# A new hand-laid order for a fused attention and token-mixing kernel

## The chip, the cores and the metric

The kernel runs on one core of a Trainium2 chip. A core has five engines with instruction queues of their own, each working strictly in order: TensorE (PE: matrix products and transposes, written to PSUM), VectorE (DVE), ScalarE (ACT), GpSimd (POOL, which does not read PSUM here), and SyncE (SP), which in this kernel issues all transfers (DMAs). The metric is the device time of one launch in microseconds. Three launches of the kernel before took 235.21, 235.92 and 237.58 us; the median is 235.92 us.

## The reference

Inputs are q, k and v (8 batches, 8 heads, 576 positions, 64 per head) and four weights. The first half is an attention in two parts whose results are added:

```python
# coarse: means over 4 neighbouring positions, full softmax over 144, result repeated 4 times
out_up = np.repeat(sm_attn(q_d, k_d, v_d), 4, axis=2)
# local: softmax over the positions with |i - j| < 4
mask = np.abs(pos[:, None] - pos[None, :]) < 4
scores = np.where(mask, 0.125 * q @ k.T, -1e9)
x = out_up + softmax(scores) @ v          # then heads are laid side by side: 8 x 576 x 512
```

The second half mixes tokens and channels:

```python
theta = x @ w_theta
y = w_tok_r @ (x * cos(theta)) + w_tok_i @ (x * sin(theta))     # over the 576 positions
u = x + y
out = u + np.maximum(u @ w_ch, 0)
```

Everything comes in and goes out as float32; inside, the kernel computes in bfloat16 with float32 sums.

## The kernel before, in words

One launch works through the eight batches. A batch is cut into steps of some tenths of a microsecond to one microsecond each, and each step has a two-letter name:

- `lk`, `lq` load a pair of heads of k or q into one of 16 staging slots (line 287); `ck`, `cq` cast it to bfloat16 (line 296); `tp` transposes it on PE (line 303), `ev` moves it from PSUM (line 316). Batch 7 is transposed by DMA instead (`dk`). `kd`, `qd` sum groups of four positions (lines 322 to 336). `lv`, `lw` load v (line 348), `cv` casts it (line 396). For batch 0, v takes another way (`l1`, `c1`, `t1`, `e1`, `x1`).
- Coarse attention: `pv`/`vd` (means of v), `sd` (scores, line 426), `ed` (exponential, line 437), `nd` (line 447), `xn` (normalising, line 458), `xd` and `xc` (transposed to xdT, lines 466 and 470).
- Local attention: `ps` (scores, line 482), `ex` (exponential, line 490), `mk` (product with the band, line 501), `po` (line 511), `nm` (normalising, lines 519 and 520), `xt` (transpose, line 533), `xa` (sum of both attentions, line 541).
- Second half: `th`, `tt` (x times w_theta, lines 552 and 564), `cs`, `ct` (cosine and sine), `xm` (x transposed, line 591), `zz`, `zt` (products), `mx` (token matrices, line 632, eight steps of nine matmuls per batch), `ua` (x + y, line 637), `up`/`uc` or `du` (u transposed by PE or by DMA), `ch` (u times w_ch, line 662), `rl` (line 667), `st` (store, line 671). The last 64 positions of two batches go together through `ut`, `dt`, `ht`, `rt`, and are stored by `sr` and `ss` (line 700).
- Weights: `la`/`ca` theta, `lb`/`cb` the token matrices with their transposes `wp`/`wc` (line 273), `lc`/`cc` the channel weight.
- `wm` issues matmuls of a constant tile whose result nobody reads (line 755): its first character is a PSUM bank, the second a number of 512-column matmuls, the third a last one in units of 64 columns. `te` and `ts` make ACT load the table of the exponential or of the sine early (line 761). `k0` does nothing.

A string, `ORDER`, holds 1,191 such words and is the whole schedule. The program takes the words one by one; each kind of word goes through its batches and parts by itself (the first `tp` is batch 0's first, and so on), and what stands behind the two letters says where: a letter v, a or g is the engine (DVE, ACT, POOL), a digit or two are PSUM banks, and for loads a character is the staging slot:

```python
    for word in ORDER.split():
        kind, place = word[:2], word[2:]
        ...
        STEPS[kind][0](*next(todo[kind]), place)
        pin()
```

`pin()` ties each instruction to the one before it on the same engine, so every engine's queue, SP's too, has exactly the order of the words. Between engines the waits come from the data: a step starts when its inputs are there and its buffer or bank is free. In the text, `tp111` is the `tp` step of batch 1, head group 1, q (the last digit is 0 for k, 1 for q), and `lq13` the fourth load of q of batch 1.

Of the kernel before, what the change touches and what calls it, by code (L numbers as in the profile page):

```python
# [67 lines left out]
lv9 tp23 nm ts cs cqa th4 lq7 xm5 xt01 th6 evv cs tp23 xa zz cqa tt4 ua tp01 kdg cs ct cqg evv ztv th5 lw evv lw xm7
zz cs tp23 mx6 xm4 kdg zp5 qdg ua eva zz cvv ps01 cqa ps23 lv8 xm7 kdg zz zcv lk4 te ex lw mx6 mx4 ua mx5 sd01 mkv lvb
lw ua ex po67 mkv cva ps23 qdg lca lcc utg ed lce nm mx4 cvg ex lcd lvf ua lk1 po01 lk2 sd67 lw po23 ckg nm cqa nm mx5  # L70
ckg ed tp01 cvg ua lq5 eva tp67 mx4 lq0 cca ua up5 evv cvg ua ccg ccg pv23 mkg ucv vda lk3 qdv ps01 ps67 ex up4 mx5
ccv nd23 ex ua nd01 uca kdg ch5 po67 xn ps23 ckg cka lv9 mx4 xn tp01 lw ex mkg rl nm lk6 cva ckg xd5 sd23 ua cqg xcv
# [12 lines left out]
po01 ch4 zz lw cs nm zz ztg ch7 te ex dz xd6 ch5 cvg rl lw lqe utg rl mkg po01 ps23 st mx4 lw lkd up7 cqg cka st ex
up2 uca nm ch3 rl xt01 kdg st st cvg xcv cva qdg ckg ua xa mkg uca po45 pv67 mx2 nm mx0 ua lk6 sd45 vda lk2 rl lq7
xt67 cqg ua ps23 xa mx1 lv5 ed po45 ua lq3 nm st mkv cqg dt ex dk9 sd23 xt67 ckg ed mx0 mkg du xa nd45 ch1 ckg ua po23
xn po67 th0 ts cs th4 tt5 nm cs nd23 rl dkf nm ct cqg evg dka xm1 xm0 mx6 zz th1 th7 cs dk1 cs xm4 xm5 zz ztv xn ua zz
mx6 zz mx4 po23 ua dz xt01 po67 xd5 ua xcv eva lw evg mx4 nm st mx5 eva du xa mx2 ht3 qdg ua mx4 xt01 ua kdg nm ua utg
ps67 du rt cvv du st ps23 kdg ua te ex ex mx5 mx4 ps67 lvb lv0 lw lw qdv xa lv8 sd23 cva xt01 ua mkv xa mkg mx5 ex st  # L90
lv4 ua po67 ua ed nm sd01 ed po23 mkg cvg ch4 ch5 mx0 nm tt1 lw lw cvg cvg rl sr po67 rl dxd po23 ua nm po45 nm ts ct
nm th0 pv67 th1 dx vda ch2 ztg nd45 st st nd67 du xn du xn cs cs du th3 cs th0 xd1 xt45 xt67 rl xcv cs xt23 xa utg dxc
ch1 dx zz ch0 ch4 xa ss ch5 dz th6 zz ch7 dt du xa tt2 zz th3 dxe dx zz st cs rl th1 mx6 cs mx3 ct st ua rl ztv rl cs
dx7 dx mx2 th6 ht4 rt zz mx1 ua mx0 cs rl mx3 mx6 zz dz rl zz ua ua zz mx7 mx1 mx2 ua ua mx0 ua mx3 ua mx6 ua ua mx1
st ua du mx0 st mx2 ua ss utv ch3 ua ua ua st ua utv ch2 ch1 ch0 ch7 ch6 du ch4 du du du du st rl sr rl du du rl dt
ch1 st st rl st rl st st rl rl ht0 rl st st rm su rt sr ss st
"""


# [699 lines left out]
```

## Time and profile before

| what | value |
|---|---|
| three launches, us | 235.21, 235.92, 237.58 (median 235.92) |
| profiled execution: span, us | 232.1 |
| median less the profiled span, us | 3.8 |
| PE busy | 220.7 us (95%), of which 40 dummies of 512 columns are 10.6 us |
| DVE, ACT, POOL busy | 191.8, 156.1, 135.5 us |
| DMA queue of the kernel | 84.6% of 16 engines' time, 48.81 MB |
| transfers issued by SP | 197 plain and 36 transposes |

The profile shows one execution. The page gives its span alone, from the first to the last instruction; what lies around it is in the timed launches only. A row of the page's groups reads: line, engine, operation, tile written, tiles read, shape, count, then the busy time of the group and the mean of one in ns, then the idle time of the engine just before, with what ended it. Busy time counts overlapping instructions once; PE's matmuls overlap their neighbours, so a mean is longer than the spacing.

### The profile page before, as it was taken

The page shows a single profiled execution, that of the slowest core. Times are in us where ns is not written, and L with a number is a line of the kernel's source. Part 1 is how long each engine was busy: PE and PEld are TensorE (multiplying, and loading weights), DVE is VectorE, ACT ScalarE, POOL GpSimd, SP SyncE. Part 2 cuts the span into 40 slices and gives each one's busy share as a digit, 9 for nine tenths or more (in the row PEclk, how much of TensorE's full clock was granted, in tenths as well). Part 3 has the DMA queues.
Part 4 walks back from the last instruction along what each step waited for, and adds up shares of the span by engine and source line. Part 5 has one row for each costly group of instructions (what it writes and reads, how often), then busy time and mean ns, then how long its engine had stood idle before and what let it go on. Part 6 is the DMA issues. An engine that isn't in the chain of part 4 may idle for free.

```text
span 232.1 us, 9462 instructions
## 1 busy us (share of the span) xinstructions
PE 220.7 (95%) x3986; PEld 153.2 (66%) x3986; DVE 191.8 (83%) x365; ACT 156.1 (67%) x241; POOL 135.5 (58%) x179
## 2 busy tenths in 40 slices
PE   7998899999998999999999999999999998999991
PEld 2665678777776765776768766676676563767750
DVE  6699999989997988868997997799889967567572
ACT  3359999799877989867976979857766591620000
POOL 7468989869999656897472837767386510000000
PEclk9999999999999999999999999999999999999998
DMA  6999989999999899989606895899957766556676
GB/s 204 382 392 390 298 134 252 365 263 193 264 263 195 224 290 208 203 209 210 174 3 178 226 234 147 293 249 173 153 122 189 144 138 100 154 126 182 138 235 217
DMA packets 76795, 49.41 MB, mean 213 GB/s; under 512 B 61136, under 2 KB 61392, under 8 KB 76752
## 3 DMA queue, kind: packets, MB, share of 16 engines
q1 hardware_dynamic: 76752, 48.81, 84.6%
q8 instruction: 31, 0.51, 1.1%
q14 instruction: 12, 0.10, 0.2%
HBM read 33.98 MB, written 9.44 MB: 187 GB/s over the span
## 4 chain that ended last, share of the span: by engine, by line
PE 72%; DVE 12%; DMA 5%; SPq 3%; issue 3%; ACT 2%; DVEq 0%
PE PS L632 24%; PE PS L662 10%; PE PS L552 9%; PE PS L303 5%; PE PS L755 4%; PE PS L511 3%; DVE xT L541 3%; DMA out_dram<-osb 2%; DVE pm L501 2%; PE PS L591 2%; PE PS L482 2%; DMA st<-xT 2%; SPq L641 2%; PE PS L533 2%; DVE uT L637 2%
## 5 line engine op out<-in xcount | busy, mean ns | idle before, releaser
L632 PE MATMUL PS<-WT,z 128*128 128x288 bf16 x576 | 77.9, 286 | 1.7 <-issue 1.7
L632 PEld LDWEIGHTS <-z 128*128 128x128 bf16 x576 | 53.8, 98 | 17.5 <-issue 2.8
L637 DVE TENSOR_TENSOR uT<-PS,xT 128x288 bf16<-128x288 f32 x64 | 28.1, 450 | 11.4 <-PE PS L632 11.1
L552 PE MATMUL PS<-wth,xT 128*128 128x512 bf16 x128 | 32.3, 380 | 0.7 <-DVE xT L541 0.7
L557 ACT ACTIVATE cs<-PS,pihc 128x512 bf16<-128x512 f32 x32 | 22.3, 696 | 15.1 <-PE PS L552 9.9
L662 PE MATMUL PS<-wch,uT 128*128 128x512 bf16 (+1 forms) x132 | 30.6, 373 | 0.0
L520 DVE TENSOR_TENSOR tmp<-PS,rl 128x512 bf16<-128x512 f32 x40 | 27.7, 692 | 1.4
L541 DVE TENSOR_TENSOR xT<-PS,xdT 128x928 bf16<-128x928 f32 (+1 forms) x24 | 22.7, 952 | 3.4 <-PE PS L533 3.1
L490 ACT ACTIVATE pm<-PS 128x1024 bf16<-128x1024 f32 (+1 forms) x24 | 20.4, 877 | 7.0 <-PE PS L482 2.7
L501 POOL TENSOR_TENSOR pm<-pm,band 128x1024 bf16<-128x1024 bf16 (+1 forms) x13 | 22.2, 1709 | 2.9 <-ACT pm L490 2.9
L667 DVE SCALAR_TENSOR_TENSOR osb<-PS,ur 128x512 f32<-128x512 f32 (+1 forms) x33 | 21.8, 669 | 2.4 <-PE PS L662 1.6
L330 POOL TENSOR_TENSOR two<-kT 128x580 f32<-128x580 bf16 x15 | 17.5, 1163 | 6.1 <-ACT kT L316 5.2
L296 POOL CAST q_tm<-st 128x576 bf16<-128x576 f32 x22 | 14.4, 664 | 10.8 <-DMA st<-in_q_dram 10.8
L662 PEld LDWEIGHTS <-uT 128*128 128x128 bf16 x132 | 12.2, 98 | 12.2 <-issue 0.3
L558 ACT ACTIVATE cs<-PS 128x512 bf16<-128x512 f32 x32 | 19.4, 605 | 0.0
L330 POOL TENSOR_TENSOR two<-qT 128x576 f32<-128x576 bf16 x11 | 12.8, 1167 | 10.5 <-ACT qT L316 7.1
L552 PEld LDWEIGHTS <-xT 128*128 128x128 bf16 x128 | 11.2, 98 | 10.7 <-issue 1.3
L616 DVE TENSOR_TENSOR z<-PS,cs 128x1024 bf16<-128x1024 bf16 x24 | 16.2, 685 | 1.9 <-PE PS L591 0.9
L437 ACT ACTIVATE pd<-PS 128x864 bf16<-128x864 f32 x16 | 14.1, 889 | 5.2 <-PE PS L426 5.2
L761 ACT ACT_TABLE_LOAD x13 | 16.7, 1283 | 0.2
L296 POOL CAST k_tm<-st 128x576 bf16<-128x576 f32 x21 | 14.4, 695 | 1.4 <-DMA st<-in_k_dram 1.4
L396 POOL CAST v_w<-st 128x512 bf16<-128x512 f32 x21 | 13.3, 653 | 1.3 <-DMA st<-in_v_dram 1.2
(119 smaller groups left out, 419.3 us busy)
## 6 DMA issues: line engine op xcount, KB each, us to landing
st<-in_q_dram SPq DMA_DIRECT2D x32, 288.0 KB, 6.3
st<-in_k_dram SPq DMA_DIRECT2D x32, 288.0 KB, 6.0
st<-in_v_dram SPq DMA_DIRECT2D x70, 128.0 KB, 4.7
out_dram<-osb SPq DMA_DIRECT2D x31, 256.0 KB, 2.9
out_dram<-osb SPq DMA_DIRECT2D x10, 128.0 KB, 2.4
st<-in_v_dram SPq DMA_DIRECT2D x4, 288.0 KB, 3.7
st<-in_moe_w_tok_r_dram SPq DMA_DIRECT2D x4, 288.0 KB, 6.2
st<-in_moe_w_tok_i_dram SPq DMA_DIRECT2D x4, 288.0 KB, 7.2
```

The lines of the kernel that those rows point to most:

```text
L296: COPY[w](out=to[:, r, :], in_=of[:, r, :])
L330: nc.gpsimd.tensor_tensor(out=t, in0=src[:, :, 0:2], in1=src[:, :, 2:4], op=ALU.add)
L490: nc.scalar.activation(out=pm[(3 * b + u) % NPM][:, :, 0:n].rearrange("p e c j w -> p e (c j w)"), in_=at.pop(("ps", b, u))[:, :, 0:4 * W ...
L501: EW[w].tensor_tensor(out=t, in0=t, in1=m, op=ALU.mult)
L520: nc.vector.tensor_tensor(out=tmp[(NCH * b + c) % NTMP].rearrange("p g (j d) -> p g j d", d=D), in0=ps[:, :, :, 0:D], in1=r.unsqueeze(3).t ...
L541: nc.vector.tensor_tensor(out=xT[b % 2][:, :, lo:lo + cnt].rearrange("p e (m j) -> p e m j", j=4), in0=at.pop(("xt", b, u))[:, :, 0:cnt].r ...
L552: nc.tensor.matmul(out=ps, lhsT=xT[b % 2][:, dc, P * c:P * c + P], rhs=wth[:, dc, :], start=(dc == 0), stop=(dc == 3))
L557: nc.scalar.activation(out=t[:, 0, :], in_=ps, func=AF.Sin, bias=pihc, scale=1.0)
L632: nc.tensor.matmul(out=ps, lhsT=z[b % 2][:, j, P * dc:P * dc + P], rhs=WT[:, j, cols], start=(j == 0), stop=(j == 8))
L637: nc.vector.tensor_tensor(out=uT[b % 2][:, dc, cols], in0=at.pop(("mx", b, i)), in1=xT[b % 2][:, dc, cols], op=ALU.add)
L662: nc.tensor.matmul(out=ps[:, cols], lhsT=uT[b % 2][:, dc, P * c:P * c + P], rhs=wch[:, dc, cols], start=(dc == 0), stop=(dc == 3))
L667: nc.vector.scalar_tensor_tensor(out=o[:, cols], in0=at["ch", b, c][:, cols], scalar=0.0, in1=ur[b % 2][:, c, cols], op0=ALU.max, op1=ALU.add)
```

## The change

Only the string `ORDER` is another one. It has the same 1,191 words in number, and the same steps, with these differences that can be counted:

| words | before | after |
|---|---|---|
| `wm` (dummies) | 8: 40 x 512 + 1,984 columns | 6: 24 x 512 + 1,152 columns |
| `te`, `ts` (table loads) | 6, 7 | 7, 8 |
| `ck`, `cq` on DVE / ACT / POOL | 1 / 20 / 43 | 12 / 15 / 37 |
| `cb` on DVE / ACT / POOL | 0 / 1 / 8 | 2 / 0 / 7 |
| `cv` on DVE / ACT / POOL | 8 / 11 / 21 | 7 / 12 / 21 |
| `mk` on DVE / POOL | 11 / 13 | 9 / 15 |
| `kd`, `qd` on DVE / POOL | 6 / 26 | 5 / 27 |
| `xc` on DVE / ACT | 7 / 1 | 2 / 6 |
| `uc` on DVE / ACT | 6 / 10 | 8 / 8 |
| `ev` on DVE / ACT / POOL | 9 / 21 / 2 | 8 / 21 / 3 |

The loads of q, k and v, the weights and the stores are issued in another order and into other slots. Of the 16 slots the new order uses 14. The start, a part of the middle and the end of the diff:

```diff
@@ -55,45 +55,45 @@
 ORDER = """
-l10 l11 l12 c1v c1a c1g k0 l13 kcv wm061 t101 c1g lq4 e1v wm256 t123 lk5 lk6 kca e1v wm483 x12 x13 lk7 ckv lq8 x10 cka
-lq9 x11 tp45 kcg cqa cva cqg x16 cqg lka cvv cvv lqb evv cvv ckg cva lkc kdg cka cqa lqd ckg lke laf wm772 tp23 evv
-wm754 tp67 pv45 tp01 qdv kcg eva vdv la0 kdg lq1 eva cka wm256 ps23 ex ps67 lk2 qdv ps01 mkv wm446 sd45 sd23 ex ed
...
-cbg lw cbg cqg lw xa xm1 nm th6 xt23 lv6 evv th7 ts cs xa zz tp45 cbg cbg wp0 cs wcv lv3 xm6 cs tt2 xm3 th7 wp1 lw xm0
-zz zz lw qdv lk8 wcv eva ct lk4 lq9 cs cbg cbg cbg cbg wp6 wca wp3 wp2 wp4 wp5 wca wp1 wcv wcv wcv wp2 ztg ps67 ps45
...
-ch1 st st rl st rl st st rl rl ht0 rl st st rm su rt sr ss st
+l10 l11 l12 c1a c1v c1a wm760 t101 l13 c1a wm765 t123 e1v e1a kcv kcv lk4 lk5 ckg lq6 cqg lq7 lk8 ckv wm735 tp01 x12
+kcg kcg x13 x14 x15 eva cvv lk0 x16 lq9 lq1 cqg wm720 tp01 ckg lq2 cvv lk3 lk4 ckg cva cva kdv cva cqg pv23 eva lq5
+cqv tp45 tp01 evv la6 qdg lka kdv vda eva wm752 ps01 la8 ps23 ckg cka ex qdv tp45 mkv cag ex cqv wm726 sd67 cqg ed mkg
...
+xca ckg ckg xt23 mkg tp01 lb6 lb2 xa xt67 caa ts lb5 po45 cbg th2 lb8 xa nm cbg cbg cbg evv cs xm3 xm7 th6 cs cbg xt45
+cbv th2 cs lb0 wp0 wp6 xa wcv wca cbg cbg wp1 zz lq1 tt4 kdg lqa th0 lv9 wp6 cbv lv4 wp5 wp3 ct wcv lv3 cqg cqg cs
+tp12 lv6 lw eva lw lw lw zz wcv lv2 lw xm4 xm6 wp7 wcv ztg wcv lka lk1 lq0 lq8 zz zp0 zca wp5 wp4 lk5 qdg zz qdg wcv
...
+rl st st ch0 rl st st st rl rm st st su ht7 rt sr ss k0
 """
```

Around the tail stores of the first two batches the old order reads `ht0 cka ed rt ... ps67 ss ...` with `sr` much later, the new one `ht7 ex up6 lv3 uca rt sr up0 ...` with `ss` much later.

More of the change, by code (lines that the diff above doesn't have):

```diff
@@ L68 @@
[L68 to L72, printed above, removed]
@@ new lines @@
+ztv lcb eva tp23 zz ucv zp5 th4 cs ckg lv1 lw lv2 lvc ckg xm6 evv mx0 cka cs te zcv xm7 tp12 ckv zz zz qdg kdg cvv lw
+ps34 ex ua ps56 ex mx7 qdg evv mkv ua mx0 ua cca cqg tp12 eva up5 ucv mx7 ua po56 sd01 lw mx2 kdg cvg sd34 cva cvg lc4
+ed nm mkv ps01 lc5 ua ex po56 ed cvv cvg up7 lq6 lk3 lk8 uca lq1 lva lw mx2 ccv lq2 lqb nm po01 po34 nm lv7 pv56 mx7
+lk9 nm tp01 cvg lkc lv0 ua lw lw ccv mkg vda nd56 nd23 xn xn eva ua mx4 ua ps01 ps56 po23 nm xd7 cca ch4 xcv rl qdg ex
+ex xt01 cqv sd23 ed ps67 xa lv6 lv5 lv4 lvd ex mkg mx5 ua cqv xt23 xt67 xa po01 nm lw lw xa th4 kdg ckg ch5 lw rl cva
@@ new lines @@
+ts up3 th2 cs xm4 xm7 ckv ckv ckg up6 uca tt3 cs lqc st tp01 zz utg uca th2 th4 evv zz ct po56 st sd01 lq9 nm lv8 xm3
+cs cs te lk3 xm2 ch7 zz lk1 rl cvg cvg pv45 ed ztg zz lk0 lk7 up3 zp6 zca cqg ch7 ch2 st cqa uca vdv rl lw tp01 rl eva
+st nd45 cva tp67 xn nd23 xn cvv lw tp01 qdg cqv lqc ch5 st rl st ch2 eva xd7 eva mkg mkg po01 po56 xca rl nm nm ps34
+ex kdg qdg mx2 mx0 mkg ua ua ps67 lv5 cva lk4 ex xt23 xa sd45 ckg mx0 utv xt67 xa po23 ua nm cvg cvg ed sd45 cqa ed ts
+kdg lq3 mx1 ua tp67 evv th0 cs mx2 th1 xt67 ua lv9 lw cqa cs lv8 po45 cqg xa nm lw lw pv02 vda xm3 mx7 qdg ua zz tt4
@@ new lines @@
+th0 nd23 xn ct xm7 th1 dt zz lvc lw ckg cs xm0 nd23 tp67 tp45 lq3 lqd lq6 cs lk1 lkb up1 mkg lq2 lva eva xn xm2 cvg
+lv5 zz eva te zz ucv mx3 ua po67 po01 nm nm ztv qdg ps45 st xd2 ex mkv lw mx3 cqa ua ch7 xt01 ps56 ps34 rl xca ex xa
+zp2 zcv ht7 ex up6 lv3 uca rt sr up0 ucv st ch1 utg po67 kdg sd23 ed sd45 ed cqg cka ckv ch0 nm lw rl mkg ps67 lk7 lkd
+ex po23 ckg lw mx1 nm po23 cvg cva ts po45 xt67 rl cvg ua xa mx0 mkg nm nm th1 lv4 lv9 lw lv8 lvc up7 ua cs ucv cva
+mx2 mx3 xt01 ua po45 cqg pv27 ckg nm xa lq0 ua ckg ckv ch6 rl cqg ss vda tp45 tp01 dk7 eva evv th7 cs qdg nd23 lq2
@@ new lines @@
+tp45 eva xm6 lw tp01 lw xm7 xn cva th2 zz zz eva evg tt3 ct cs xm7 nd56 xn mx0 ua zz th3 mx0 ztv ps12 ua ps67 cs po34
+nm lqa kdg cqa te cqg xm0 mx5 zz cvg ex ua mx3 up5 ex kdg xd4 up2 up1 ch0 ua mkg st st ch3 uca lw xca qdv rl uca sd45
+ed lv5 lw ucv xt67 dz xa xt01 utg mx2 cka lq0 xa cvg mx7 mx0 lv7 cvv rl ps34 ex cvg cvg sd56 ed ua ua ua po12 st mx7
+nm st ua xt01 xa lv8 mkg po56 nm pv23 vda up7 ch4 mkg cqa cqg mkv dkc lkd ckg up0 uca ts ucv lv4 ch5 nd23 dkd dka nd67
+rl tt4 ct rl th5 cs du du xn po01 po23 xn po67 nm nm evg eva th4 th5 evg xm3 xm2 zz nm th0 cs cs ztg zz xm1 mx3 mx4 ua
@@ new lines @@
+ua xm2 xd3 xcv mx7 qdg lw cs te po34 lw lw zz zz dz ps56 ex xt01 ua xa ht2 nm mx7 ua utv ps01 ps34 ex ex xt56 xa mx7
+ua ch0 rl cva dt mx7 xt01 rt sr xa mkg cva ts cvg ua kdg po34 po56 st du st mx2 tt7 nm du nm mx0 ua ua mx6 kdg qdg
+sd45 mkv po23 cvv st st sd01 ct te ed ed nm mx7 mx5 pv01 ua ztg ua po67 mkg po23 ua mx5 ua dx4 du ss du du dx nm ch4
+rl dx7 nm vda ts nd01 xn th5 cs th7 cs nd23 xn ch4 rl ch0 xd7 dx xt12 xt34 xt56 xca rl xa xa xa zz dz zz st st uta th0
+du ch7 ch1 ch2 dt cs zz tt0 th6 ct th5 th0 ch3 ch4 rl cs zz th6 mx7 rl st ua ztg cs rl mx5 ht7 mx2 mx1 dx5 dx cs cs
```

35 lines of the change are left out of this document (7 added, 28 removed).

## The prediction

> **What bounds the kernel now.** I read the page first: its busy line, and the DMA lines in 40 slices of 5.80 us.
>
> ```profile
> span 232.1 us, 9462 instructions
> PE 220.7 (95%) x3986; PEld 153.2 (66%) x3986; DVE 191.8 (83%) x365; ACT 156.1 (67%) x241; POOL 135.5 (58%) x179
> DMA  6999989999999899989606895899957766556676
> GB/s 204 382 392 390 298 134 252 365 263 193 264 263 195 224 290 208 203 209 210 174 3 178 226 234 147 293 249 173 153 122 189 144 138 100 154 126 182 138 235 217
> ```
>
> TensorE (PE) is busy for 95% of the span, but the DMA digits stand at 8 or 9 from 5.8 to about 104 us. The averages hide which of the two leads where, so I next read the stretches: microseconds, then busy time (instructions) of PE, PE's weight loads, DVE, ACT and POOL, the granted clock, the DMA share and GB/s.
>
> ```profile
> 20.00:35.00 15.00, 13.26 (x329) 10.19 (x328) 14.49 (x28) 14.95 (x24) 13.06 (x17) 1.00 0.98 253
> 35.00:50.00 15.00, 14.96 (x396) 12.03 (x395) 13.91 (x30) 12.99 (x20) 11.82 (x16) 1.00 1.01 299
> 50.00:65.00 15.00, 14.99 (x292) 10.82 (x283) 14.54 (x23) 14.08 (x24) 14.29 (x18) 1.00 1.11 234
> 65.00:80.00 15.00, 13.87 (x373) 10.82 (x374) 13.04 (x26) 11.30 (x17) 12.72 (x16) 1.00 0.99 216
> 80.00:100.00 20.00, 19.45 (x352) 13.39 (x354) 15.95 (x34) 16.94 (x27) 15.13 (x19) 1.00 1.10 243
> 100.00:120.00 20.00, 20.00 (x373) 13.85 (x361) 17.19 (x32) 17.23 (x28) 14.79 (x20) 1.00 0.66 156
> 120.00:140.00 20.00, 19.76 (x413) 14.68 (x412) 17.83 (x31) 15.04 (x25) 9.25 (x11) 1.00 0.73 192
> 140.00:160.00 20.00, 20.00 (x428) 13.38 (x426) 16.78 (x33) 15.11 (x24) 15.12 (x19) 1.00 1.00 219
> 160.00:180.00 20.00, 19.40 (x379) 14.31 (x377) 18.09 (x31) 14.70 (x19) 12.46 (x11) 1.00 0.80 160
> 180.00:200.00 20.00, 19.21 (x298) 10.97 (x298) 15.11 (x30) 10.91 (x20) 3.71 (x6) 1.00 0.64 124
> ```
>
> Three things follow. PE has little left to win: from 35 to 200 us its idle time is 0.04 + 0.01 + 1.13 + 0.55 + 0.24 + 0.60 + 0.79 = 3.4 us. From 20 to 80 us four resources are close to full at once: the DMA engines (0.98 to 1.11), PE, and DVE with 14.49 + 13.91 + 14.54 + 13.04 = 56.0 of 60 us. And in the first 20 us PE looks full only because the order puts dummy matmuls (words `wm`, line 755) where it expects PE to wait. The granted clock is 1.00 in all of these rows, so it is no term here.
>
> **The change, part by part.** Every step runs as before, on the same tiles; what changes is the order, the engine of some copies, masks and sums, the staging slots, the PSUM banks, the number of table loads and the dummies. PE's real work is therefore the same.
>
> *Fewer dummies.* The eight old `wm` words have 40 matmuls of 512 columns and 1,984 columns in remainders, 22,464 columns; the six new ones have 24 and 1,152, so 13,440. The rate comes from two words of the old order, 8 x 512 + 192 = 4,288 and 5 x 512 + 256 = 2,816 columns:
>
> ```profile
> 8.31 1.97 PE L755 MATMUL PS<-warm 128*128 128x512 bf16 x9
> 14.27 1.35 PE L755 MATMUL PS<-warm 128*128 128x512 bf16 x6
> ```
>
> 0.62 us for 1,472 columns is 0.421 ns each, and 9,024 columns fewer are 3.8 us off PE's queue. That is worth 3.8 us only if what follows on PE is ready 3.8 us sooner.
>
> *What is late next: landings.* A load's median time to landing against the spacing of the issues tells of the queue:
>
> ```profile
> st<-in_k_dram SPq DMA_DIRECT2D x32, 288.0 KB, 6.0
> 12.28 0.33 SPq L287 DMA_DIRECT2D st<-in_k_dram  x1
> 13.03 0.33 SPq L240 DMA_DIRECT2D st<-in_moe_w_theta_dram  x1
> ```
>
> One issue in 0.75 us and 6.0 us to land means about eight transfers on the way; SP issues at the pace of the landings. Both orders issue the same 33 loads first: v, q and k of batch 0, q and k of batch 1, theta and the two token matrices (29 of 288 KB and 4 of 256 KB, 9.6 MB). In the new order PE needs the last of them (`lq13`) for the transposes `tp111`; in the old one the last is `lb8`, and POOL casts it as soon as it is there:
>
> ```profile
> L261 POOL CAST uT<-st x8: 667/669/671, 27.7 to 32.7; 128x576 bf16<-128x576 f32 x8
> L296 POOL CAST q_tm<-st 128x576 bf16<-128x576 f32 x22 | 14.4, 664 | 10.8 <-DMA st<-in_q_dram 10.8
> 34.12 2.32 PE L273 MATMUL PS<-ident,uT 128*128 128x128 bf16 x40
> 51.16 0.50 PE PS L303 x9
> 138.32 0.22 PE PS L591 x4
> ```
>
> The last of the 33 is there at about 32.7 us, with a DMA share of 0.98 in that stretch, so the new order can't have it sooner; with a cast of 0.66 us, `tp111` starts at 33.4 us at the earliest. When does the old order have as much PE work behind it? At 34.12 us it starts its last seven `wp` steps (2.32 us for eight groups of five, 0.28 each without the last one's tail). The new order has four of these behind it at `tp111` and is short of `tp111` (0.50) and of two `xm` (0.22 each): 4 x 0.28 - 0.50 - 0.44 = +0.2, so 34.3 us. PE's lead is then at most 34.3 - 33.4 = 0.9 us: 2.9 of the 3.8 us come back as waiting for DMA. Ends for this term: 0 (POOL reaches the same cast at about the same time, as it has mask, weight casts and `kd10` ahead of it) and 3.8 (the landings are not what ends the wait).
>
> [...]
>
> *Work moved to DVE.* DVE gets 12 instead of 1 of the casts of k and q and two of the token casts; it gives up five `xc`, three `qd` and two of eleven masks, and takes two `kd`. These even out within a few us over the run. What doesn't is that casts and masks read and write SBUF alone, and such DVE steps are slow beside POOL:
>
> ```profile
> L501 DVE TENSOR_TENSOR pm<-pm,band x11: 417/1050/2192, 20.0 to 177.3; 128x1024 bf16<-128x1024 bf16 x9, 128x512 bf16<-128x512 bf16 x2
> 19.97 0.69 DVE L501 TENSOR_TENSOR pm<-pm,band 128x1024 bf16<-128x1024 bf16 x1
> L396 DVE CAST v_w<-st x5: 410/793/1266, 38.0 to 173.6; 128x512 bf16<-128x512 f32 x5
> L396 POOL CAST v_w<-st x21: 603/609/1072, 39.2 to 181.6; 128x512 bf16<-128x512 f32 x21
> 9.90 0.53 DVE L296 CAST k_tm<-st 128x512 bf16<-128x512 f32 x2
> ```
>
> The mask at 19.97 us took 0.69, the median is 1.05 and the worst 2.19; the v cast took 0.41 to 1.27, median 0.79. An excess of about 0.4 us a step is the nearest row for the moved casts (0.53 alone). Steps of this kind on DVE (`mk`, `ck`, `cq`, `cv`, `ca`, `cb`, `cc`, `c1`, `zt`, `ut`) go from 26 to 37, and in the first 90 us of PE's own work from 13 to 25. Twelve at 0.4 are 4.8 us; ends 0 (each falls where POOL is quiet) and 4.8. DVE is free for 4.0 us from 20 to 80 us, so I take nothing on the path, and the whole 4.8 as the slow end.
>
> *Waits inside.* I leave the 3.4 us between 35 and 200 us as they are, with ends 0 and double. Two further table loads (one `te`, one `ts`) are ACT's; ACT is busy for 47.4 of 60 us from 100 to 160 us, so I take nothing, and they cost a load each only where they fall between a matmul and a product that PE waits for.
>
> *SP's queue.* The old order makes SP wait at the tail store `ss0` for a result:
>
> ```profile
> SPq L700 <- DVE rd L457: 10.9, 1, 10.9
> ```
>
> All later loads and stores queue behind it on SP. In the new order the first tail store, `sr0`, stands right behind the same result `rt0`, with 138 transfers ahead of it instead of 127; eleven at the 0.75 us of an issue are 8 us, so SP arrives nearer to the result. PE idles for only 0.24 us from 100 to 140 us, so the gain is none; nor is there a cost, should SP be early again, as that wait was covered before.
>
> *The end.* In the old order three stores follow the last vector step, in the new one two:
>
> ```profile
> 227.08 0.69 DVE L695 SCALAR_TENSOR_TENSOR osb<-PS,utr 128x512 f32<-128x512 f32 x1
> 227.80 1.12 SPq L700 DMA_DIRECT2D out_dram<-osb  x2
> 228.97 0.59 SPq L671 DMA_DIRECT2D out_dram<-osb  x1
> ```
>
> The last issue comes one step of 0.6 us sooner behind `rt3`: 0.6 us, ends 0 and 0.6.
>
> **Sum.** 232.1 - 0.9 - 0.6 = 230.6 us of span. The timed runs' median lies 235.92 - 232.1 = 3.8 us over the profiled span; carried over, 234.4 us, 0.6% less.
>
> **The rivals.** *The landings don't hold.* If the new queue order keeps the DMA engines fuller in the first 10 us (share below one there: first digit 6) or the cast at 32.7 was late for POOL's sake, the 3.8 us stay: 235.9 - 3.8 - 0.6 = 231.5. If the waits inside shrink by half too, 229.8. For it: POOL is busy 13.06 of 15 us in that stretch. Against it: DMA share 0.98 to 1.11 right through.
>
> *DVE takes the lead.* Twelve more steps that POOL can stall, in a stretch where DVE has 4.0 us to spare, and that spare is mostly waiting for PE's results, which doesn't move. Then each normalisation, product and sum behind a stalled cast is late and PE waits for banks. Price 4.8 us, less the 1.5 above: 235.9 + 3.3 = 239.2. It decides once DVE from 20 to 80 us is above 97% busy. For it: the rows of the masks. Against it: the new order also takes masks from DVE, and the steps may have been put where POOL rests. [...]
>
> *The order changes nothing*: it would then stay at 235.9 less the 3.8 us, which is the first rival; no separate case.
>
> **How the numbers follow.** A measurement of this kernel can tell about 1% from no change (235.21 to 237.58 in three runs), so the bounds are 233.6 and 238.3. The forecast (the lead is eaten by landings, little else changes) has 0.42, the first rival 0.36, the second 0.22. Faster 0.36, same 0.42, slower 0.22; the likeliest time is 234.4. The range takes in the first rival down to half of its further gain, 230.0, and the second nearly to its price, 239.0; the forecast's own range is 233 to 237.
>
> **What would show it.** Dummies: line 755 with 30 instead of 48 matmuls. Landings: the transposes of line 303 before 35 us preceded by PE idle time that ends with a cast, `tp111` at 33 to 34 us, DMA share near 1.0 up to 100 us. DVE: 20 to 80 us at 56 to 58 us busy, casts of line 296 on DVE near 0.6 us; 0.9 or more each, with over 58 us, speaks for the second rival. Waits: PE idle from 35 to 200 us near 3.4 us. End: two stores behind the last vector step. I am wrong if `tp111` starts before 32 us, or if PE loses more than 7 us after 35 us.

## The result and the profile after

| | before | after |
|---|---|---|
| median of four launches each, us | 235.56 (234.45 to 237.58) | 243.53 (243.26 to 246.44) |
| ratio after to before | | 1.034, 95% interval 1.024 to 1.044 |
| profiled span, us | 232.1 | 241.6 |

The new order is 3.4% slower. The forecast was 234.4 us, in a range that ended at 239.0. The profiled launch of the new order took 243.26 us, 1.7 us more than its span, and so did every later launch; so 1.7 us lie around a span here. The 3.8 us that the forecast added to the old order's span were mostly the distance of a quick launch to the median. Medians are over all launches of a series, while ratios leave out launches over 1.5% above the fastest of the same kernel, so the two need not agree to the last digit.

The page of the changed kernel, with the same rows as before:

```profile
span 241.6 us, 9385 instructions
PE 217.3 (90%) x3937; PEld 152.9 (63%) x3966; DVE 197.4 (82%) x382; ACT 159.9 (66%) x246; POOL 140.4 (58%) x173
PEclk9999799999999999999999999999999999999998
DMA  6999889997999999868937779955406656837877
```

PE's busy time is no longer than before (some matmul records are missing), so PE does not work more, it waits more. New is the 7 in the fifth digit of the clock. The stretches show where (us, then busy time of PE, weight loads, DVE, ACT, POOL, clock, DMA share, GB/s):

```profile
20.00:35.00 15.00, 11.25 (x278) 8.70 (x277) 14.13 (x24) 10.54 (x17) 12.78 (x17) 0.89 0.86 253
35.00:50.00 15.00, 14.59 (x321) 12.05 (x320) 13.39 (x29) 13.76 (x21) 11.70 (x15) 1.00 0.99 298
50.00:65.00 15.00, 14.11 (x307) 10.81 (x307) 14.64 (x27) 13.71 (x23) 13.96 (x17) 1.00 0.88 225
65.00:80.00 15.00, 14.53 (x365) 11.14 (x365) 13.60 (x31) 11.12 (x17) 9.85 (x12) 1.00 1.00 241
80.00:100.00 20.00, 18.12 (x327) 12.06 (x330) 19.81 (x38) 17.55 (x28) 15.41 (x17) 1.00 0.98 238
100.00:120.00 20.00, 19.53 (x411) 14.54 (x402) 15.93 (x32) 16.69 (x26) 13.54 (x15) 1.00 0.85 227
120.00:140.00 20.00, 17.64 (x384) 11.92 (x388) 18.04 (x36) 13.63 (x23) 12.14 (x15) 1.00 0.65 151
140.00:160.00 20.00, 18.80 (x379) 14.39 (x381) 16.30 (x28) 14.38 (x23) 18.21 (x19) 1.00 0.89 202
160.00:180.00 20.00, 19.74 (x407) 13.66 (x416) 17.49 (x35) 17.02 (x26) 11.63 (x10) 1.00 0.39 78
180.00:200.00 20.00, 19.48 (x350) 12.87 (x352) 16.62 (x31) 11.62 (x21) 5.84 (x6) 1.00 0.58 127
```

From 35 to 200 us PE is idle for 0.41 + 0.89 + 0.47 + 1.88 + 0.47 + 2.36 + 1.20 + 0.26 + 0.52 = 8.5 us, 5.1 more than before. Matching the start of each step of PE's own work in the two traces gives the rest, to about half a us at most places: the new order is 1.7 us ahead at 17 us, about 1 behind at 28, 1.5 to 1.8 at 34, 4 at 88, 6 to 8 at 131, 6 at 212, 8 at 234, and 9.5 at the end. Three places stand out: 17 to 28 us, 80 to 131 us, and the end from 212 us.

**The first place.** The timeline of the new order there, by engine (start, length, line):

```profile
19.33 2.47 POOL L501 TENSOR_TENSOR pm<-pm,band 128x1024 bf16<-128x1024 bf16 x1
19.75 2.86 DVE L296 CAST q_tm<-st 128x512 bf16<-128x512 f32 x2
22.75 0.69 DVE L520 TENSOR_TENSOR tmp<-PS,rl 128x512 bf16<-128x512 f32 x1
23.49 0.32 PE L482 MATMUL PS<-qT,kT 64*64 64x64 bf16 x16 [2.85 <-DVE tmp L520]
```

One cast on DVE (`cq10`, pieces of eight rows and of one) takes 2.86 us while GpSimd has a mask in hand. Behind it in DVE's queue stands the normalisation `nm00`, which frees the PSUM banks that the scores `ps02` are to be written to, and PE waits for it for 2.85 us. What that does to the clock shows if the trace is cut at the two steps of the clock (24.74 and 28.15 us):

```profile
21.33:24.74 3.41, 1.25 (x39) 1.21 (x39) 3.07 (x7) 0.88 (x2) 3.21 (x6) 1.00 0.89 262
24.74:28.15 3.41, 3.38 (x89) 2.98 (x87) 3.08 (x8) 2.71 (x4) 3.41 (x6) 0.50 1.01 345
```

In 3.41 us PE was busy for 1.25, and the next 3.41 us it had half the clock: up to 1.7 us more, for a wait that was over.

**The casts as a group**, with the mask and the v casts on DVE. The first two rows are total busy time and mean in ns, the others shortest, median and longest:

```profile
L296 DVE CAST q_tm<-st 128x512 bf16<-128x512 f32 (+1 forms) x12 | 9.5, 832 | 0.3 <-DMA st<-in_q_dram 0.3
L296 DVE CAST k_tm<-st 128x512 bf16<-128x512 f32 (+1 forms) x12 | 5.6, 514 | 0.8 <-DMA st<-in_k_dram 0.8
```

```profile
L501 DVE TENSOR_TENSOR pm<-pm,band x9: 417/724/1360, 18.9 to 183.7; 128x1024 bf16<-128x1024 bf16 x6, 128x512 bf16<-128x512 bf16 x3
L396 DVE CAST v_w<-st x5: 410/467/1882, 64.1 to 185.0; 128x512 bf16<-128x512 f32 x5
```

Twelve casts in 24 pieces, 12 x 0.832 + 12 x 0.514 = 16.2 us, so 1.35 a cast; the old order's one VectorE cast took 0.43 + 0.19 = 0.62. The excess is 0.73 each, 8.7 us in all. The piece of one row is stalled too: it took from 0.18 to 1.14 us, and the piece of eight rows from 0.42 to 2.34.

**The end.** Waits of PE, of SP's queue over the whole span and of DVE from 200 us (total, times, longest), and the last steps:

```profile
PE PS L632 <- DVE uT L637: 1.7, 2, 1.3
SPq L700 <- DVE osb L695: 8.3, 1, 8.3
DVE z L611 <- DMA st<-xT: 4.3, 1, 4.3
```

```profile
235.28 1.46 DVE L667 SCALAR_TENSOR_TENSOR osb<-PS,ur 128x512 f32<-128x512 f32 x3 [1.03 <-DMA out_dram<-osb]
236.74 0.69 DVE L695 SCALAR_TENSOR_TENSOR osb<-PS,utr 128x512 f32<-128x512 f32 x1
237.69 1.13 SPq L700 DMA_DIRECT2D out_dram<-osb  x2
```

SP waits 8.3 us at the tail store `sr1` (171 to 180 us), later DVE waits 4.3 us for the transposed x of batch 7 and PE with it, and at the very end DVE waits for a store to free an output tile.

### The profile page after: what moved, and what is told of

The parts are those of the page before. It is cut to its first block, busy times and chain, and to the rows that moved or that the text cites. A ratio compares the mean times of both kernels' runs of the same rounds, so it can differ in the third digit from the quotient of the medians.

```text
span 241.6 us, 9385 instructions
## 1 busy us (share of the span) xinstructions
PE 217.3 (90%) x3937; PEld 152.9 (63%) x3966; DVE 197.4 (82%) x382; ACT 159.9 (66%) x246; POOL 140.4 (58%) x173
## 4 chain that ended last, share of the span: by engine, by line
PE 70%; DVE 17%; issue 6%; DMA 4%; SPq 1%; ACT 0%; DVEq 0%
PE PS L632 23%; PE PS L552 11%; PE PS L662 9%; PE PS L303 5%; DMA st<-in_q_dram 3%; DVE q_tm L296 2%; PE PS L591 2%; PE PS L511 2%; DVE osb L667 2%; PE PS L533 2%; DVE tmp L520 2%; PE PS L447 2%; PE PS L482 2%; DVE uT L637 2%; DMA out_dram<-osb 2%
## 5 line engine op out<-in xcount | busy, mean ns | idle before, releaser
L632 PE MATMUL PS<-WT,z 128*128 128x288 bf16 x576 | 77.4, 286 | 2.1 <-DVE uT L637 1.7
L632 PEld LDWEIGHTS <-z 128*128 128x128 bf16 x576 | 54.4, 98 | 17.7 <-issue 2.2
L501 POOL TENSOR_TENSOR pm<-pm,band 128x1024 bf16<-128x1024 bf16 (+1 forms) x15 | 27.9, 1865 | 7.9 <-ACT pm L490 7.8
L552 PE MATMUL PS<-wth,xT 128*128 128x512 bf16 x115 | 30.7, 379 | 1.9 <-DVE xT L541 0.7
L662 PE MATMUL PS<-wch,uT 128*128 128x512 bf16 (+1 forms) x120 | 29.3, 372 | 1.5 <-DVE osb L667 0.7
L330 POOL TENSOR_TENSOR two<-qT 128x576 f32<-128x576 bf16 x14 | 16.3, 1165 | 15.5 <-ACT qT L316 7.4
L761 ACT ACT_TABLE_LOAD x15 | 19.2, 1283 | 0.3
L558 ACT ACTIVATE cs<-PS 128x512 bf16<-128x512 f32 x32 | 19.2, 599 | 0.0
L573 POOL TENSOR_TENSOR zT<-xT,cst 128x512 bf16<-128x512 bf16 x5 | 6.3, 1264 | 21.9 <-DMA z<-zT 15.7
L330 POOL TENSOR_TENSOR two<-kT 128x580 f32<-128x580 bf16 x13 | 15.5, 1190 | 1.6 <-DVE kT L316 0.6
L652 POOL COPY ut<-uT 128x256 bf16<-128x256 bf16 x4 | 1.8, 444 | 24.7 <-DVE uT L637 24.7
```

The costliest lines, as they stand in the source:

```text
L330: nc.gpsimd.tensor_tensor(out=t, in0=src[:, :, 0:2], in1=src[:, :, 2:4], op=ALU.add)
L501: EW[w].tensor_tensor(out=t, in0=t, in1=m, op=ALU.mult)
L552: nc.tensor.matmul(out=ps, lhsT=xT[b % 2][:, dc, P * c:P * c + P], rhs=wth[:, dc, :], start=(dc == 0), stop=(dc == 3))
L632: nc.tensor.matmul(out=ps, lhsT=z[b % 2][:, j, P * dc:P * dc + P], rhs=WT[:, j, cols], start=(j == 0), stop=(j == 8))
L662: nc.tensor.matmul(out=ps[:, cols], lhsT=uT[b % 2][:, dc, P * c:P * c + P], rhs=wch[:, dc, cols], start=(dc == 0), stop=(dc == 3))
```

## The experiments

Theories. *Port*: a VectorE copy within SBUF stands still beside GpSimd, the steps queued behind it are late, and PE pays. *Queue*: SP's wait makes the last transposes late. *Landings*, the forecast's own: PE waits for loads. A fourth, *code*, came out of the first four runs. Ratios are to the old order in the same series of runs, with 95% intervals; a span is that of the one profiled launch. The new order was timed in the first series alone, and the old order's median was 235.6, 237.3, 236.1, 236.7 and 237.0 us in the five series, so a distance to the new order's 243.5 us is known to a us or two, and single spans of like kernels differ by about 1 us. Words are changed in `ORDER` unless said.

**One cast to ScalarE (one_cast).** The cast of the first place alone:

```diff
-cqv tp45 tp01 evv la6 qdg lka kdv vda eva wm752 ps01 la8 ps23 ckg cka ex qdv tp45 mkv cag ex cqv wm726 sd67 cqg ed mkg
+cqv tp45 tp01 evv la6 qdg lka kdv vda eva wm752 ps01 la8 ps23 ckg cka ex qdv tp45 mkv cag ex cqa wm726 sd67 cqg ed mkg
```

> Of the new order one word is changed: the cast of q of batch 1, heads 0 and 1 (on VectorE from 19.7 to 22.6 us, 2.9 us long beside a GpSimd mask) goes to ScalarE. Port theory (a VectorE step that reads and writes SBUF stands still beside GpSimd, and PE pays for it): PE's idle time from 20 to 24 us falls from 3.0 us to 1.2 or less, the granted clock from 20 to 35 us is 1.00 instead of 0.89, and 2.5 to 3.5 us come back: 240.0 to 241.0 us. Landing theory (PE waits for loads there, whoever casts): PE's idle time and the time stay, 243.5 within 0.7. If the stall at 20 us has no weight because later waits eat it, the dip goes but the time is above 242.5.

242.06 us, 1.033 (1.015 to 1.050), span 240.3. PE's wait for `nm` in front of `ps02` fell from 2.85 to 0.34 us, and at 34 us PE was 0.4 us ahead of the old order instead of 1.5 behind. But the half clock came all the same, and the gain was gone by 74 us. The largest of the waits that took it is again one for a normalisation, now behind another VectorE step, the cast of a weight `wch`:

```profile
70.75 1.37 DVE L243 CAST wch<-st 128x512 bf16<-128x512 f32 x1
73.02 0.40 PE L404 MATMUL PS<-v_w,pu 128*32 128x512 bf16 x4 [0.88 <-DVE tmp L520]
```

At 79 us PE also stopped inside the scores `ps32`, for 1.4 us against 0.6 in the new order. The cast `cq10` was the cause of the first wait, which fell as port theory says; the time did not: 242.06 misses the 240 to 241 that were expected, and comes nearer to the case in which the stall has no weight (above 242.5).

**All casts to ScalarE, or in one piece (casts_act, casts_whole).** The first changes 12 words (`ckv`, `cqv` to `cka`, `cqa`), the second only the cast's code:

```diff
-            for r in ((slice(0, WR - 1), slice(WR - 1, WR)) if w == "v" else (slice(0, WR),)):
+            for r in ((slice(0, WR - 1), slice(WR - 1, WR)) if w == "n" else (slice(0, WR),)):
```

> All 12 VectorE casts of k and q in the new order go to ScalarE, in place. Port theory: the excess of these casts, 8.7 us on VectorE, is gone and so are the PE waits beside them (20, 80 to 85 and 126 us); 4 to 6 us come back, 237.5 to 239.5 us. If ScalarE pays for it instead (8 us more work on an engine that is busy for 66%), half of that: 239.5 to 241.5. Landing theory: 243.5 within 1.

> The 12 VectorE casts of k and q stay on VectorE but are issued in one piece of nine rows instead of pieces of eight and one. The work is the same, the instruction's shape another. [...] If any SBUF step of VectorE is stalled by GpSimd, the one piece is stalled as long as the two together (mean 1.34 us for both): 243.5 within 1.

casts_act: 241.05 us, 1.026 (1.008 to 1.044). casts_whole: 241.04 us, 1.023 (0.999 to 1.047), span 239.2. In whole rows the casts are still on DVE, at the same places in its queue:

```profile
L296 DVE CAST k_tm<-st x6: 734/743/753, 9.9 to 136.9; 128x576 bf16<-128x576 f32 x6
L296 DVE CAST q_tm<-st x6: 741/742/746, 14.4 to 99.6; 128x576 bf16<-128x576 f32 x6
```

All twelve take 0.73 to 0.75 us, whatever GpSimd does, and at the first place nobody is stalled:

```profile
19.66 0.75 DVE L296 CAST q_tm<-st 128x576 bf16<-128x576 f32 x1
19.88 2.12 POOL L501 TENSOR_TENSOR pm<-pm,band 128x1024 bf16<-128x1024 bf16 x1 [0.85 <-ACT pm L490]
21.29 0.32 PE L482 MATMUL PS<-qT,kT 64*64 64x64 bf16 x16 [0.33 <-DVE tmp L520]
```

So it is the instruction's shape that gets stalled, not VectorE's work. In the new order's trace the four eight-row pieces beside which GpSimd was idle took 0.42 to 0.43 us, the eight with GpSimd at work beside them 0.42 to 2.34; of the one-row pieces the four with GpSimd idle took 0.19 us, the others 0.18 to 1.14. The nine-row casts pay 0.12 us (0.74 to 0.62), and none of the twelve was stalled. What in the shape decides was not shown.

Both medians are 2.5 us under the new order's, where port theory had asked for 4 to 6 us of casts_act and 3 to 5 of casts_whole: both missed it, and casts_act's lies in the range of its other case, in which ScalarE pays. (The intervals of this series are wide; the launches of casts_whole, 238.1 to 243.1 us, all lie below the new order's 243.3 to 246.4.) By PE's steps casts_whole was 2.2 us ahead of the new order at 34 us, 0.8 at 78, and 2.3 behind at 82. So part of the gain went in small waits, and the rest at 79 us, in both kernels, with another 3.4 us at half clock (casts_whole):

```profile
78.78 0.26 PE L482 MATMUL PS<-qT,kT 64*64 64x64 bf16 x12
81.89 0.22 PE L482 MATMUL PS<-qT,kT 64*64 64x64 bf16 x4 [2.85 <-issue]
```

```profile
82.37:85.79 3.42, 3.42 (x74) 2.02 (x73) 1.56 (x3) 2.43 (x4) 2.15 (x5) 0.50 0.81 162
```

PE stops in the middle of a step: 12 of the 16 matmuls of `ps32` are done, the other four need nothing new, and the release is "issue", nothing that the profile shows. The trace has packets of 16 KB on an instruction queue, 31 in a launch (0.51 MB in the page's row of that queue). Their bytes over PE's 7,945 recorded instructions (matmuls, weight loads and 13 of its sequencer) are 64 for each, so by this estimate a packet holds 256 of them. One of the packets starts at 79.17 us. And PE stops at the same number in run after run: 3,009 recorded instructions in one_cast, casts_act, casts_whole, and 1,985, four packets earlier, inside the step `tt1`. Where no records are missing, every such stop, the old order's too (at 2,753 and 3,777), comes at 193 plus a multiple of 256. Hence the code theory: PE has run through what is loaded. In casts_whole PE runs through the 256 instructions in front of the stop in 2.4 us, from 76.4 us on; the next packet starts 2.75 us after PE enters this block.

**The late tail store (sr_late).**

```diff
-ua ch0 rl cva dt mx7 xt01 rt sr xa mkg cva ts cvg ua kdg po34 po56 st du st mx2 tt7 nm du nm mx0 ua ua mx6 kdg qdg
-sd45 mkv po23 cvv st st sd01 ct te ed ed nm mx7 mx5 pv01 ua ztg ua po67 mkg po23 ua mx5 ua dx4 du ss du du dx nm ch4
+ua ch0 rl cva dt mx7 xt01 rt xa mkg cva ts cvg ua kdg po34 po56 st du st mx2 tt7 nm du nm mx0 ua ua mx6 kdg qdg sd45
+mkv po23 cvv st st sd01 ct te ed ed nm mx7 mx5 pv01 ua ztg ua po67 mkg po23 ua mx5 ua dx4 du sr ss du du dx nm ch4
```

> In the new order one word is moved: the tail store sr1, which makes SP wait from 171 to 180 us, goes to the place right ahead of ss1. Queue theory (what stands behind sr1 on SP, 14 stores and transposes, is late, and the end is late through it): SP's longest wait is under 4 us, the wait of GpSimd for a transposed zT (15.7 us) shrinks by 5 or more, and 1 to 2 us come back: 241.5 to 242.5 us. If SP catches up before anyone needs these transfers: 243.5 within 0.6, as in the old order, where the wait of 10.9 us cost nothing that I saw.

244.85 us, 1.043 (1.027 to 1.060), no gain, and outside what either case expected. SP's queue shows why:

```profile
SPq L601 <- DVE uT L637: 7.4, 1, 7.4
```

SP now stands at line 601, the transpose `dx60`, until 186.5 us. That writes a staging slot that the cast `cv74` on DVE still reads until 186.4. The wait had a second holder: it was moved and not removed, so the run does not say what it costs.

**Dummies, and a long step, in front of the stop (whole_dummy, whole_mx17).** Both on casts_whole. One puts `wm6a0` (ten matmuls of 512 columns) ahead of `ps32`, the other moves the eighth token product of batch 1:

```diff
-ex xt01 cqv sd23 ed ps67 xa lv6 lv5 lv4 lvd ex mkg mx5 ua cqv xt23 xt67 xa po01 nm lw lw xa th4 kdg ckg ch5 lw rl cva
+ex xt01 cqv sd23 ed mx5 ps67 xa lv6 lv5 lv4 lvd ex mkg ua cqv xt23 xt67 xa po01 nm lw lw xa th4 kdg ckg ch5 lw rl cva
```

> The new order with whole-row casts on VectorE, and ten dummy matmuls of 512 columns (2.1 us of PE work) put right ahead of the scores ps32, at 79 us. With whole rows alone PE stood still inside ps32 from 79.0 to 81.9 us, with nothing in the trace to wait for but a 16 KB packet of PE's instruction queue that started at 79.2 us, and the next 3.4 us ran at half clock. Code theory (PE has used up its loaded instructions; 256 of them went in 2.4 us): the dummies fill the hole, the stop inside ps32 falls from 3.1 us to 1.1 or less, no window at half clock follows, and the span falls by about 1.7 us although 2.1 us of work are added: 237.5 us against 239.2. If PE waits there for data or the stop comes with the step: the 2.1 us are added, 241.3 us of span.

> The new order with whole-row casts, and the token product mx17 (1.1 us for 18 instructions) moved from behind ps32 to ahead of it, so that PE does longer work between two instruction packets. Code theory: the stop inside ps32 falls from 3.1 us to about 2.0, PE's busy time from 79 to 82.4 us rises above half, and with the half clock gone 2 to 3 us come back: span 236.5 to 237.5 us against 239.2. If the half clock stays: about 1 us. If the stop is not about instructions: 239.2 within 0.7.

whole_dummy: 240.63 us, 1.024 (1.015 to 1.033), span 238.5, with 2.1 us of useless work added and no half clock before the end:

```profile
76.13 2.33 PE L755 MATMUL PS<-warm 128*128 128x512 bf16 x10
78.40 0.22 PE L482 MATMUL PS<-qT,kT 64*64 64x64 bf16 x2
79.34 0.31 PE L482 MATMUL PS<-qT,kT 64*64 64x64 bf16 x14 [0.72 <-issue]
```

The ten dummies are 20 instructions, and the stop has moved by 20: it comes after 2 matmuls of `ps32` instead of 12, again at number 3,009. That is what code theory says and no wait for data would do. The stop fell from 2.85 to 0.72 us. The span fell by 0.7 and not by 1.7, as PE lost 1.7 us at 212 us in this run. whole_mx17: 240.0 us, 1.017 (1.010 to 1.025), span 236.8; the stop came after 3 matmuls (18 instructions less) and took 0.37 us, without a half clock.

**The queue with both holders moved (late_queue), and with whole rows (whole_late).** late_queue is sr_late with `cv74` on GpSimd (`po23 cvv st` to `po23 cvg st`); whole_late adds whole rows and `cv63` on ScalarE.

> The new order as it is, with the tail store sr1 moved to ss1 as before, and the cast cv74 (VectorE, 185.0 to 186.4 us, whose staging slot the transpose dx60 writes next) on GpSimd. With sr1 moved alone, SP waited for that cast at dx60 from 180.2 to 186.5 us instead. Queue theory: dx60 is issued before 182 us, the transposes of batch 7 four us or more sooner than at 211, PE's stops at mx66 (1.5 us) and ch72 (0.8) are gone, and 2 to 3 us come back: 240.5 to 241.5 us. If the end is set by PE's own work and SP has slack: 243.5 within 0.6.

> All three together in the new order: whole-row casts, the late tail store with cv74 on GpSimd, and cv63 (VectorE, 1.9 us long at 155 us beside GpSimd) on ScalarE. If the causes are separate their gains add: 2.5 for the casts, 2 to 3 for the queue, up to 1.2 for cv63, so 237 to 239 us. If time given back in one place is lost in the next (as at ps32), not under 240.

late_queue: 242.81 us, 1.030 (1.020 to 1.039), span 240.8: above the 240.5 to 241.5 that were expected, and not clear of the new order. `dx60` was issued at 185.5, not before 182. The stop in `ps32` took 2.7 us in this run, so that all was 1.5 us late, and SP still waited at `dx60`, now for `cv74` itself, which stands behind other steps of GpSimd (the same row is in whole_late):

```profile
SPq L601 <- POOL v_w L396: 3.0, 1, 3.0
```

But PE's stop of 1.3 us at `mx66`, where it had waited with DVE for the transposes of batch 7, was gone. whole_late: 237.60 us, 1.011 (1.004 to 1.018), span 236.1, which is 3.1 under casts_whole. Not all of it belongs to the three moves: by PE's steps whole_late was 1.3 us ahead of casts_whole at 155 us already, before the first of them acts, though the two orders are the same to there. That leaves some 1.9 us for `cv63` and the queue together; no run separates the two. PE was idle for only 0.6 of the 135 us from 85 to 220 us. What was left were the two stops for code, and the half clock behind one of them:

```profile
PE PS L482 <- issue: 2.6, 1, 2.6
PE PS L564 <- issue: 1.0, 1, 1.0
```

**All of it (all_fix).** whole_late with `mx17` ahead of `ps32` and, in the same way, `th11` ahead of `tt1`:

```diff
-xt34 ckg cqg xt67 xa cka ts xa mx5 ua th0 ua cs xm3 xm4 tp67 tt2 ct evv zz lw lw lva lw lv8 lw th5 tp01 cqv up6 cs th7
+xt34 ckg cqg xt67 xa cka ts xa mx5 ua th0 ua cs xm3 xm4 tp67 th5 tt2 ct evv zz lw lw lva lw lv8 lw tp01 cqv up6 cs th7
```

> The new order with everything that the runs so far point to: whole-row casts on VectorE, cv63 on ScalarE and cv74 on GpSimd, the late tail store sr1, mx17 ahead of ps32, and the product th11 (0.9 us for 8 instructions) moved ahead of tt1, inside which PE stopped for 1.1 us at 53.6 us with its inputs there. Without the last two moves the span was 236.1 us, with a stop of 2.8 us inside ps32 and 3.4 us at half clock behind it. Code theory: both stops fall under 0.8 us, no half clock, and 3 to 4.5 us come back: span 231.5 to 233, 233 to 235 us in time, level with the old order or up to 1% faster. If the two moves only shift the stops: 236.1 within 0.7 of span.

237.22 us, 1.0043 (0.9999 to 1.0087), profiled span 233.6: level with the old order, not ahead of it, and above the 233 to 235 us that were expected. In the profile both steps run through in one piece, and no window at half clock comes before the end of PE's work:

```profile
54.53 0.63 PE L564 MATMUL PS<-xT,wth 128*128 128x64 bf16 x16
78.35 0.41 PE L482 MATMUL PS<-qT,kT 64*64 64x64 bf16 x16
```

The launches lie between 235.3 and 240.5 us and show a mean clock from 0.979 to 0.999. One window of 3.41 us at half clock takes 1.7 of some 235 us, 0.007 of the mean, and the profiled launch has 0.997, so those at 0.979 to 0.986, at least four of the twelve, lose further windows. Which, the one profile can't say. Smaller stops for code are left in it too, of 0.4 us at 99.4 and 0.5 at 118.8.

**The moves for code alone (code_only).** The two moves of all_fix in the new order, and nothing else.

> The new order with nothing but the two moves on PE: th11 ahead of tt1 and mx17 ahead of ps32; the casts on VectorE stay in pieces and sr1 stays where it is. In the new order's own trace PE stops inside these two steps for 0.8 us each, in other runs of it with one part changed for up to 2.9. If the stops for code stand for much of the result by themselves: 2 to 3 us less than 243.5, so 240.5 to 241.5. If PE comes late to these places because of the stalled casts, so that the code is there when it comes, and the stops show only once the casts are mended: 1 us or less, so 242.5 to 243.5, and the half clock at 20 to 28 us stays.

243.65 us, 1.025 (1.018 to 1.032): no clear gain, as the second case has it. The reason given there is only half right. The half clock stayed (from 24.0 us, and again from 129.8), but `ps32` stopped for 2.2 us although `mx17` stood ahead of it, against 0.37 in whole_mx17:

```profile
80.74 0.22 PE L482 MATMUL PS<-qT,kT 64*64 64x64 bf16 x3
83.14 0.29 PE L482 MATMUL PS<-qT,kT 64*64 64x64 bf16 x13 [2.17 <-issue]
```

The code packet started at 80.3 us, here late against PE's own progress, in whole_mx17 at 77.0. At `ps32` PE goes on 2.5 to 3.0 us after the packet's start in these runs; what delays the start is open. Over the nine variants with complete records, the packets that fell due while the DMA share was 1.0 or more started at a median of 2.3 us after PE entered its last loaded block (95 packets), those with a share from 0.5 to 0.8 at 1.1 us (64). That speaks for a wait behind data in the DMA engines; it wasn't tried by itself.

**The casts in the old order (before_split, before_whole).** The same 12 casts go to DVE in the old order, in two pieces and in one:

```diff
-lq9 x11 tp45 kcg cqa cva cqg x16 cqg lka cvv cvv lqb evv cvv ckg cva lkc kdg cka cqa lqd ckg lke laf wm772 tp23 evv
+lq9 x11 tp45 kcg cqa cva cqg x16 cqg lka cvv cvv lqb evv cvv ckg cva lkc kdg cka cqv lqd ckg lke laf wm772 tp23 evv
...
```

> The old order with one thing of the new: the same 12 casts of k and q (ck01, cq03, cq10, cq32, ck41, cq40, cq41, ck43, ck50, cq50, ck61, ck71) go to VectorE, in pieces of eight rows and one, from the places that they have in the old order. Port theory: the casts are stalled beside GpSimd (mean of the two pieces over 1.0 us), PE's idle time from 20 to 200 us grows, and the time rises by 2 to 5 us over the old order's. If a VectorE cast as such costs nothing on the path, as I took it: within 1 us of the old order.

> The old order with the same 12 casts on VectorE, in one piece of nine rows each. Port theory: each takes 0.74 us whatever GpSimd does, and the time lies between the old order's and 1.5 us over it, at least 1.5 us below the same casts in pieces. [...]

before_split: 251.79 us, 1.068 (1.058 to 1.077). before_whole: 241.40 us, 1.015 (1.005 to 1.025). The casts of each (13, with the one that the old order had there):

```profile
L296 DVE CAST k_tm<-st 128x512 bf16<-128x512 f32 (+1 forms) x14 | 9.3, 711 | 0.6 <-DMA st<-in_k_dram 0.6
L296 DVE CAST q_tm<-st 128x512 bf16<-128x512 f32 (+1 forms) x12 | 8.7, 767 | 0.0
```

```profile
L296 DVE CAST k_tm<-st 128x576 bf16<-128x576 f32 x7 | 5.1, 745 | 1.1 <-DMA st<-in_k_dram 1.1
L296 DVE CAST q_tm<-st 128x576 bf16<-128x576 f32 x6 | 4.5, 744 | 0.0
```

14 x 0.711 + 12 x 0.767 = 19.2 us in pieces, 13 x 0.745 = 9.7 in one. The difference of 9.5 us on DVE is 10.4 us in time between the medians and some 12 by the ratios, where 2 to 5 us over the old order had been expected of the pieces and 15 came: in this order about the whole stall of the VectorE casts goes to the path, with two windows at half clock (24.5 to 31.4 us), up to 3.4 us, on top. The casts' mere work costs some 3.6 us (ratio 1.015, interval about 1 to 6 us), over the 1.5 us that were expected at most. Landings are no rival here, as the loads and their order are the same in both; a load that starts late because a stalled cast frees its staging slot late is part of the stall's price.

## Why the prediction was wrong

**Fewer dummies: right in size, wrong in what ate it.** The dummies' busy time fell by 3.6 us (11.6 in the old order, 8.0 in casts_whole and all_fix), where the forecast had 3.8. The new order was ahead of the old one by 1.7 us at 17 us. The forecast let landings take 2.9 of the 3.8 us at `tp111`, which was to start at 33.4 us at the earliest. POOL's last q casts and `tp111` in the new order:

```profile
31.78 1.28 POOL L296 CAST q_tm<-st 128x576 bf16<-128x576 f32 x2
36.12 0.67 PE L303 MATMUL PS<-ident,q_tm 128*128 128x128 bf16 x9
```

The casts were done at 33.06, the data had landed at 31.3, and `tp111` ran 3 us later: PE was late by itself, from the first place. With whole rows `tp111` started at 33.9, and in all_fix, where the casts were done at 32.44, at 33.45 with PE busy right up to it:

```profile
31.17 1.27 POOL L296 CAST q_tm<-st 128x576 bf16<-128x576 f32 x2
33.45 0.67 PE L303 MATMUL PS<-ident,q_tm 128*128 128x128 bf16 x9
```

So no run has PE waiting for landings at that step, and the data came 1.4 us sooner than the old order's 32.7, which the forecast had held to be impossible. PE led the old order by 0.6 to 0.8 us there in the mended runs, close to the forecast's 0.9, but by luck: what ate the rest were other waits, 1.3 us of PE from 10 to 20 us in all_fix, where the old order has none.

**Work moved to DVE: the step that failed.** "DVE is free for 4.0 us from 20 to 80 us, so I take nothing on the path, and the whole 4.8 as the slow end." Two things were wrong with it. First the size: 0.4 us of excess a step came from medians of masks and v casts; the measured mean is 0.73, and in the old order's places 19.2/13 - 0.62 = 0.86. The longest steps, which the quoted rows had (2.19 us), are what PE feels. Second, the free time of an engine over 60 us says nothing of a queue that runs in order: DVE was busy for 14.13 + 13.39 + 14.64 + 13.60 = 55.8 us of the 60, less than before and under the 97% at which the rival was to decide, and yet the rival's mechanism decided. A stall of 2 us comes at one moment, and the normalisation behind it is due at that moment.

**The second rival** had the mechanism and the side, with a chance of 0.22, and a price that was too low: 239.2 us. It left out the clock. "The granted clock is 1.00 in all of these rows, so it is no term here" was true of the old order alone; one wait of 2.85 us in a window of 3.41 brought the half clock.

**Waits inside: kept at 3.4 us, measured 8.5,** over the 7 us that were named as a sign of error. Part of it are VectorE steps beside GpSimd again: with whole rows PE's idle time from 100 to 140 us fell from 0.47 + 2.36 to 0.02 us.

**SP's queue: wrong place.** The forecast followed `sr0` and asked whether SP would be early. The store that held SP was `sr1`, at 171 us, where the last transposes queue behind it. Moving it alone moved the wait to `dx60` (sr_late). With both holders moved, PE's stop of 1.3 us at `mx66` was gone, while SP still waited 3.0 us at `dx60`; what the queue was worth in time is not separated.

**The end: wrong sign, for another reason.** From the start of the last vector step to the end of the span 232.1 - 227.08 = 5.0 us before, and 241.6 - 236.74 = 4.9 after, so one store fewer behind it saved 0.1 us and not 0.6. In front of it DVE now waits 1.0 us for a store to free an output tile, where it waited 0.4 before.

**What settles the loss.** Of 8.0 us in time, the mended kernels gave back, across series and so to a us or two: whole-row casts 2.5 (241.04); 3.4 more with the queue's two holders and `cv63` moved (237.60), of which about 1.3 was there before these moves act; the moves for code 0.4 in the median and 2.5 in the profiled span. Code stops were in the old order too (the 1.7 us of `L632 <- issue` in its waits of PE: 1.1 before 72.05 us and 0.55 before 98.9), and moving the steps for code alone gave no clear gain, so they explain less of the loss than of why each repair gave less than its stall. The casts are the one part whose price is shown in both orders. That the repairs reach the old order and don't pass it, although 3.6 us of dummies are gone, stays without a full account: the 14 staging slots in place of 16, the two more table loads, the copies given to ScalarE and the other moved steps weren't tried by themselves.

## What to carry to other kernels

Price a step that a neighbour can stall by its longest case and by what stands behind it in its engine's queue, not by a median and the engine's free time; if it must stand beside GpSimd, look for a shape that isn't stalled (nine rows instead of eight cost 0.12 us here and saved up to 2). On a busy TensorE count instructions as well as microseconds: behind 256 dense ones in 2.4 us it stood for 2.85 us here (casts_whole), by the code theory because the next part of its code was not there. And after each repair look at the next place that was late: here the first gain of 2 us was gone again by 74 us.

## What the runs showed of the hardware that was not expected

- In the traces of the two orders the stretches at one clock were whole multiples of 3.413 us, but for the last of each, from the end of PE's work on (3.5 and 3.8 us at half clock): in the new order 20.48 us at full clock, 3.41 at half and 211.63 at full are 6, 1 and 62 of them, in the old order 225.28 us at full clock are 66. So the steps stand on a grid that did not begin anew with the work. A window need not be idle to bring the half clock: PE was busy for 0.37 of the one ahead of it in the new order (1.25 of 3.41 us from 21.33 us) and for 0.16 in casts_whole (0.56 of 3.41 us from 78.96 us). The new order's window with 0.60 at 127 us had full clock behind it, the one with 0.64 in one_cast (the first row below) half clock, so the busy share of the profile alone does not decide it.

```profile
19.50:22.91 3.41, 2.18 (x84) 1.75 (x84) 2.57 (x7) 3.10 (x6) 3.08 (x3) 1.00 1.02 334
22.91:26.33 3.42, 3.39 (x92) 3.00 (x89) 2.97 (x8) 2.58 (x4) 3.42 (x6) 0.50 1.04 280
```

- PE stopped in the middle of a step with all its data there, at a fixed number of instructions (1,985 and 3,009 in the variants of the new order whose records are complete; in whole_dummy 20 instructions put ahead moved the place by 20), for up to 2.85 us (casts_whole), there from before a packet of 16 KB on the instruction queue started (79.17 us) to 81.89. In the traces of the two orders PE went on 2.3 to 3.1 us after such a packet's start (old order: packets at 69.43 and 96.06 us, PE on at 72.05 and 98.90). That the next part of its code was missing is the reading that fits these runs.
- A copy on VectorE of eight rows took from 0.42 to 2.34 us in the new order, where GpSimd works beside it, a copy of nine rows 0.73 to 0.75 us in casts_whole.
